# Moving the small ScalarE copies of a fused DFT and gated-cosine kernel to just ahead of the next sine

## The chip, the cores and the metric

The kernel runs on one core of one Trainium2 chip. The metric is the device time of one execution in microseconds; the median of three executions of the kernel before is 1958.15 us (1957.54 to 1958.85). Engines are named as the profile names them: PE (matrix multiply), PEld (its weight loads), DVE (vector), ACT (scalar), POOL (GpSimd), SP (the queue that issues nearly all DMAs).

## What is computed

```python
X = np.fft.fft(x, axis=1)            # x: (8, 3008, 256) fp32
X = np.fft.fft(X, axis=2)
t = X.real.astype(np.float32).reshape(24064, 256)
h = t @ w_in                         # w_in: (256, 2048)
g = h * np.cos(h)
return (g @ w_out).astype(np.float32)   # w_out: (2048, 256)
```

## The kernel before

All matrix work is in fp32. The DFT along the sequence (3008 = 47 x 64) is split in two: a first half (`first_half`, 47-point sums, 64 output rows per matrix) and a second half (`second_half`, 64-point sums with twiddles folded into the constant matrix `BJ`). The DFT along the 256 channels is folded once into `w_in`, which gives the matrices `WC` and `WS`. The real input makes one transformed row serve two output rows: `h` and its mirror.

The main loop goes over 8 batches, 6 groups of columns in each (225 columns in the first, 256 in the others), 8 pairs of feature blocks in each group. That makes 48 steps a batch, 384 in all; a step `t` has two half steps `u` = 0 and 1, numbered `k = 2t + u`. The program is written in the order in which each engine shall take its instructions, and each engine keeps that order. In one half step:

- PE: `mm1(cur, 0)` (weights `WC`), the second matrix product `mm2` of the step five half steps back, `mm1(cur, 1)` (weights `WS`), each as two instructions for one fp32 product. Both `mm1` add to a bank of PSUM that ACT has filled beforehand, the seed.
- ACT: `act_e` (L529, writes `ew`), `act_round` of the half step before (L545), `seed` of the half step to come (L498), and `act_sin` of the half step before (L555). In two half steps out of sixteen it also takes 512 columns of a finished accumulator (`take_m`, L631).
- DVE: `dve_h` (L533), `dve_frac` (L549, between rounding and sine), `dve_g` (L559, after the sine).
- POOL: `sums` (L575 to L582), combinations of finished groups, and the large parts of the folds.

While batch b is multiplied, `transform(b+1)` spreads the transform of the next batch over the 48 steps (this happens in the first seven batches; the last batch has no batch behind it). Its parts that matter here:

- `fold(b, c, e)` (L221 on) makes sums and differences of the input rows on POOL; when `e` is 1 a small copy of the end columns follows on ACT (L234, 94x8 elements). It runs at the end of steps 7, 10, 15, 18, 23, 26, 31 and 34.
- `take_middle(b, p)` (L287): a small ACT copy of the middle column into `xm` (L289, 94x8), at the end of steps 7, 8, 9 and 10. `middle` multiplies `xm` in step 11, and ACT copies the product to `zm`.
- At the first half step of steps 12, 20, 28 and 36 a pair of chunks goes through `first_half` into two borrowed PSUM banks. `keep_z` (L276) copies each bank to `zs` on ACT (L279) and then patches four columns of it from `zm` with a small copy (L281, 64x4).
- `store_z` at the end of the same step sends `zs` to DRAM over the SP queue; `load_z` at the end of steps 23 and 39 brings it back transposed; `second_half` uses it at the end of steps 42 to 47.

The order of ACT in a half step of a pair is thus: `act_e`, `act_round`, `keep_z` of the first chunk with its patch, `seed`, `act_sin`, `keep_z` of the second chunk with its patch. The copies for fold and middle column come at the very end of a step, so between the sine of one half step and `act_e` of the next.

Of the kernel before, what the change touches and what calls it, by code (L numbers as in the profile page):

```python
# [20 lines left out]
N2 = 47  # L21
NJ = 24
NI = 32
IP = 4
NCH = NI // IP
XP = 2 * IP
# [82 lines left out]
def kernel(  # L109
# [7 lines left out]
    nc = tc.nc  # L117
# [93 lines left out]
        return ppool.tile([128, 512], FP, tag=f"H{(turn[0] + k) % 4}", bufs=1, name=name)  # L211


    xfs = {}
    xf0 = [spool.tile([128, 2 * IP * 128], FP, tag="S", bufs=3, name="xf") for _ in range(2)]
    for xf in xf0:
# [2 lines left out]
    def fold(b, c, e):  # L219
        lo = IP * (c % 2)  # L220
        xv = xs[b, c // 2].rearrange("r (i d) -> r i d", d=ND)[0 : 2 * N2, lo : lo + IP]  # L221
        if b == 0:
            xfs[b, c] = xf0[c % 2]
        elif e == 0:
            xfs[b, c] = spool.tile([128, 2 * IP * 128], FP, tag="xf", bufs=2, name="xf")
        fv = xfs[b, c].rearrange("r (e i d) -> r e i d", e=2, d=128)[0 : 2 * N2]
        (nc.gpsimd if b else nc.vector).tensor_tensor(
            out=fv[:, e, :, 1:128],
            in0=xv[:, :, 1:128],
            in1=xv[:, :, 255:128:-1],  # L230
            op=ALU.subtract if e else ALU.add,
        )
        if e:
            (nc.scalar.copy if b else nc.gpsimd.tensor_copy)(  # L234
                out=fv[:, :, :, 0].rearrange("r e i -> r i e"), in_=xv[:, :, 0:129:128]
            )

    zss = {}

# [36 lines left out]
    def keep_z(b, c, pz):  # L276
        tag, n = ("zs", 4) if b or c < 4 else ("pq", 8)
        zs = spool.tile([128, 512], FP, tag=tag, bufs=n, name="zs")
        nc.scalar.copy(out=zs, in_=pz)  # L279
        if b:  # L280
            nc.scalar.copy(out=zs[64:128, 0:512:128], in_=zm[64:128, IP * c : IP * c + IP])  # L281
        zss[b, c] = zs

    xm = cpool.tile([128, NI], FP, tag="xm", name="xm")
    zm = cpool.tile([128, NI], FP, tag="zm", name="zm")

    def take_middle(b, p):  # L287
        xv = xs[b, p].rearrange("r (i d) -> r i d", d=ND)[0 : 2 * N2]
        nc.scalar.copy(out=xm[0 : 2 * N2, XP * p : XP * p + XP], in_=xv[:, :, 128])  # L289

    def clear_middle():
        pm = borrow("pm", 1)[64:128, 0:NI]
# [75 lines left out]
    def spread_nb():  # L368
        pq, nb = ready[0, 0]
        T = _width(0)  # L370
        pn = psum("pn", "M")
        nc.tensor.matmul(pn[:, 0:T], lhsT=ones, rhs=pq[0:1, T : 2 * T], start=True, stop=True)
        nc.scalar.copy(out=nb[:, 0:T], in_=pn[:, 0:T])
# [5 lines left out]
    def transform(b):  # L379
        todo = {}  # L380

        def at(o, *call):
            todo.setdefault(o, []).append(call)

        for p in range(4):
            at(2 * p, load_x, b, p)
            at(7 + p, take_middle, b, p)
            for k in range(4):
                at(8 * p + (6, 7, 9, 10)[k], fold, b, 2 * p + k // 2, k % 2)
            pairs[per * (b - 1) + 8 * p + 12] = b, 2 * p  # L390
            for c in (2 * p, 2 * p + 1):
                at(8 * p + 12, store_z, b, c)
        middles.add(per * (b - 1) + 11)
        at(23, load_z, b, 0)
        at(39, load_z, b, 1)
        for g in range(NG):
            at(42 + g, second_half, b, g)
        return todo
# [3 lines left out]
    def fold_weights(e, n, tag="M"):  # L402
        keep_weights(e, n, weights(e, n, tag))

    def weights(e, n, tag="M"):
        pw = psum("pw", tag)
        for i in range(2):
            nc.tensor.matmul(  # L408
                pw,
                lhsT=CS[i][:, 128 * e : 128 * e + 128],  # L410
                rhs=wr[n // 2][i][:, 512 * (n % 2) : 512 * (n % 2) + 512],
                start=(i == 0),
                stop=(i == 1),
            )
        return pw
# [8 lines left out]
    def weight_row(n):  # L424
        row = WS[0:1, 512 * n : 512 * n + 512]
        pw = psum("pw", "M")
        for k in range(4):
            nc.tensor.matmul(
                pw[:, k : k + 1],
                lhsT=row[:, 128 * k : 128 * k + 128],  # L430
                rhs=ones[:, 0:1],
                start=True,
                stop=True,
            )
        return pw
# [66 lines left out]
    def seed_first(h):  # L502
        s, T = h.s, h.s.T
        nc.tensor.matmul(
            h.H[:, 0:T],
            lhsT=wrow[:, 128 * h.u : 128 * h.u + 128],
            rhs=s.pq[0:1, T : 2 * T],
            start=False,
            stop=True,
            skip_group_check=True,  # L510
        )

    def mm1(h, e):
        s, T = h.s, h.s.T
        W = WS if e else WC
        f = 2 * s.fp + h.u
        nc.tensor.matmul(  # L517
            h.H[:, 0:T],
            lhsT=W[:, 128 * f : 128 * f + 128],
            rhs=s.pq[:, e * T : e * T + T],  # L520
            start=False,
            stop=True,
            skip_group_check=True,
        )

    def act_e(h):
        T = h.s.T
        h.ew = spool.tile([128, 256], FP, tag="ew", bufs=2, name="ew")
        nc.scalar.mul(out=h.ew[:, 0:T], in_=h.H[:, 0:T], mul=2.0)  # L529
# [290 lines left out]
    def step(t, last=None):  # L820
        s = steps[t] if 0 <= t < n else None
        return s if s is not None and (last is None or s.fp == 7) else None
# [3 lines left out]
    def unit(k):  # L826
        return halves[k] if 0 <= k < 2 * n else None
# [7 lines left out]
    for k in range(2 * n + LAG):  # L835
        t, u = divmod(k, 2)
        d, v = divmod(k - LAG, 2)
        cur, prev, old, nxt = unit(k), unit(k - 1), unit(k - 2), unit(k + 1)
        done = step(d)
        full = step(d if v else d - 1, True)  # L840
        if cur:
            if k % (2 * per) == 0:
                todo = transform(cur.s.b + 1) if cur.s.b + 1 < NB else {}
            if k not in range(3, AHEAD):
                mm1(cur, 0)
                if t == 0:
                    seed_first(cur)
                act_e(cur)
            if k == 0:
                spread_nb()  # L850
                fold_weights(1, 3)
            elif k == 1:
                pw = weights(0, 3)
            elif k == 2:
                pw = weight_row(3)
        pair = None if u else pairs.pop(t, None)
        if pair:
            b, c = pair
            pz = [first_half(b, c, borrow("pz"))]
        if old:  # L860
            dve_g(old)
            if old.u:
                sums(old.s)
        if pair:
            pz.append(first_half(b, c + 1, borrow("pz", 1)))
        pm = clear_middle() if u and t in middles else None
        if done:
            order = (0, 1, 5, 4, 3, 2, 6) if done is steps[-1] else range(7)
            mm2(done, 4 * v, 4 * v + 3, order)
        if pm is not None:  # L870
            middle(pm)
        if full and full is not steps[-1]:
            take_m(full, 1 if v else 3, nc.vector)
        if nxt and 0 < k < AHEAD - 1:
            seed(nxt)
        if prev:
            act_round(prev)
        if pm is not None:
            nc.scalar.copy(out=zm[64:128], in_=pm)
        if pair:  # L880
            keep_z(b, c, pz[0])
        if nxt and k >= AHEAD - 1:
            seed(nxt)
        if full and full is not steps[-1]:
            take_m(full, 0 if v else 2, nc.scalar)
        if prev:
            dve_frac(prev)
        if k + 1 in range(3, AHEAD):
            mm1(nxt, 0)
            act_e(nxt)  # L890
        if prev:
            act_sin(prev)
        if pair:
            keep_z(b, c + 1, pz[1])
        if k == 1:
            keep_weights(0, 3, pw)
        elif k == 2:
            keep_wn(3, pw)
        if cur:
            mm1(cur, 1)  # L900
        if done and v == 0:
            mm2(done, 3, 4, order)
        if cur:
            dve_h(cur)
        if u == 0:
            continue
        for i in range(6):
            s = step(t - 4 - i, True)
            if s:
                combine_m(s, i)  # L910
        for sg, lag in ((0, 8), (1, 10)):
            s = step(t - lag, True)
            if s:
                store_out(s, sg)
        for call in opening.pop(t, ()):
            call[0](*call[1:])
        for call in todo.pop(t % per, ()):
            call[0](*call[1:])
# [31 lines left out]
```

## Time and profile before

| | |
|---|---|
| median of three executions | 1958.15 us |
| the profiled execution, its own time | 1957.18 us |
| its span, first to last instruction | 1955.4 us |
| mean granted PE clock | 0.999 |
| PE busy | 1940.8 us, 99% |
| PEld busy | 1686.2 us, 86% |
| ACT busy | 1516.3 us, 78% |
| DVE busy | 1455.8 us, 74% |
| POOL busy | 1396.4 us, 71% |
| L234 copies on ACT (fold) | 56, mean 192 ns |
| L289 copies on ACT (middle column) | 28, mean 191 ns |
| L281 copies on ACT (patch of z) | 56, mean 194 ns |

The span and some 1.8 us around it make up the time of an execution. PE is busy almost throughout, and a busy PE can still lose time: the record of a matmul grows when its weights arrive late. The weight loads on PEld are shown by themselves, with the time that they stood idle and what ended it.

### The profile page before, as it was taken

How to read it: one execution, taken by the hardware profiler on the slowest of the kernel's cores; microseconds unless marked ns; L12 is line 12 of the kernel's file. 1: busy time of each engine (PE TensorE's matmuls, PEld its weight loads, DVE VectorE, ACT ScalarE, POOL GpSimd, SP SyncE). 2: the span in 40 equal slices, each digit the busy share in tenths (PEclk: the TensorE clock that was granted, in tenths of full speed). 3: DMA queues.
4: the chain of work that ended last, by engine and by line, in shares of the span. 5: the costliest groups of instructions: out<-in, count | busy, mean ns of one | idle time of the engine just before them, and what ended most of it. 6: DMA issues, size and time to landing. Idle time of an engine off the chain costs nothing.

```text
span 1955.4 us, 29697 instructions
## 1 busy us (share of the span) xinstructions
PE 1940.8 (99%) x9262; PEld 1686.2 (86%) x9262; DVE 1455.8 (74%) x2529; ACT 1516.3 (78%) x3450; POOL 1396.4 (71%) x1593
## 2 busy tenths in 40 slices
PE   9999999999999999999999999999999999999998
PEld 4888888888988889888898888988889888898887
DVE  3767777777777777777777777777777777788886
ACT  3777778777787787877778787788777877778775
POOL 3777767787577876787667776687767777666775
PEclk9999999999999999999999999999999999999999
DMA  8511124011230223201241111411114111100001
GB/s 199 126 32 39 23 54 78 21 36 39 49 68 18 41 41 64 47 22 40 41 80 29 38 28 41 86 24 41 27 36 86 23 38 28 38 22 16 12 16 28
DMA packets 176690, 88.70 MB, mean 45 GB/s; under 512 B 103303, under 2 KB 173622, under 8 KB 174902
## 3 DMA queue, kind: packets, MB, share of 16 engines
q1 hardware_dynamic: 176374, 86.68, 21.5%
q8 instruction: 75, 1.23, 0.3%
q14 instruction: 81, 0.66, 0.1%
q10 hardware_dynamic: 160, 0.13, 0.0%
HBM read 49.50 MB, written 37.27 MB: 44 GB/s over the span
## 4 chain that ended last, share of the span: by engine, by line
PE 97%; DMA 1%; ACT 0%; DVE 0%; SPq 0%; issue 0%; POOL 0%; POOLq 0%; ACTq 0%
PE M L608 58%; PE H L517 33%; PE pz L253 3%; PE pb L341 2%; DMA xp<-in_x_dram 1%; PE pw L408 0%; DMA wr<-in_moe_w_in_dram 0%; DMA nb<-nd 0%; DMA nd<-pq 0%; PE pz L250 0%; PE pm L298 0%; PE pd L464 0%; DVE r L549 0%; ACT H L498 0%; ACT r L555 0%
## 5 line engine op out<-in xcount | busy, mean ns | idle before, releaser
L575 POOL TENSOR_TENSOR S<-r 128x512 f32<-128x512 f32 (+1 forms) x383 | 474.8, 1240 | 453.0 <-DVE r L559 408.1
L555 ACT ACTIVATE r<-r 128x512 f32<-128x512 f32 (+1 forms) x768 | 477.5, 622 | 257.4 <-DVE r L549 254.5
L549 DVE SCALAR_TENSOR_TENSOR r<-r,H 128x512 f32<-128x512 f32 (+1 forms) x768 | 518.9, 676 | 199.0 <-ACT r L545 174.6
L559 DVE SCALAR_TENSOR_TENSOR r<-H,r 128x512 f32<-128x512 f32 (+1 forms) x768 | 519.2, 676 | 132.5 <-ACT r L555 92.5
L608 PE MATMUL M<-S,VX 128*128 128x256 f32 (+1 forms) x2304 | 615.7, 376 | 0.0
L608 PEld LDWEIGHTS M<-S,VX 128*128 128x128 f32 x2304 | 435.8, 190 | 70.9 <-issue 22.7
L517 PE MATMUL H<-pq,WC 128*128 128x256 f32 (+1 forms) x1536 | 455.7, 378 | 3.1 <-ACT H L498 2.9
L517 PE MATMUL H<-pq,WS 128*128 128x256 f32 (+1 forms) x1536 | 451.5, 376 | 0.0
L545 ACT ACTIVATE r<-H 128x512 f32<-128x512 f32 (+1 forms) x768 | 447.6, 583 | 0.0
L533 DVE TENSOR_TENSOR H<-ew,H 128x256 f32<-128x256 f32 (+1 forms) x768 | 324.8, 423 | 140.5 <-PE H L517 81.6
L608 PE MATMUL M<-r,w 128*128 128x256 f32 (+1 forms) x1536 | 387.8, 375 | 0.0
L498 ACT ACTIVATE H<-nb,wn 128x256 f32<-128x256 f32 (+1 forms) x766 | 365.8, 478 | 2.7 <-DMA nb<-nd 1.3
L529 ACT ACTIVATE ew<-H 128x256 f32<-128x256 f32 (+1 forms) x768 | 287.3, 374 | 98.2 <-PE H L517 94.4
L608 PEld LDWEIGHTS M<-r,w 128*128 128x128 f32 x1536 | 300.4, 197 | 27.0
L517 PEld LDWEIGHTS H<-pq,WC 128*128 128x128 f32 x1536 | 279.3, 190 | 50.1 <-ACT H L498 18.0
L517 PEld LDWEIGHTS H<-pq,WS 128*128 128x128 f32 x1536 | 290.2, 190 | 33.3 <-ACT ew L529 1.1
L581 POOL TENSOR_TENSOR S<-S,r 128x256 f32<-128x256 f32 (+1 forms) x383 | 275.5, 719 | 30.0
L582 POOL TENSOR_TENSOR S<-r,S 128x256 f32<-128x256 f32 (+1 forms) x383 | 274.5, 717 | 30.0
L608 PE MATMUL M<-S,w 128*128 128x256 f32 (+1 forms) x768 | 225.4, 375 | 0.0
L608 PE MATMUL M<-r,VX 128*128 128x256 f32 (+1 forms) x768 | 225.4, 375 | 0.0
L608 PEld LDWEIGHTS M<-S,w 128*128 128x128 f32 x768 | 150.6, 196 | 14.5
L608 PEld LDWEIGHTS M<-r,VX 128*128 128x128 f32 x768 | 146.0, 190 | 14.4
(74 smaller groups left out, 925.9 us busy)
## 6 DMA issues: line engine op xcount, KB each, us to landing
out_dram<-ob SPq DMA_DIRECT2D x728, 32.0 KB
xp<-in_x_dram SPq DMA_DIRECT2D x56, 256.0 KB
zd<-zs SPq DMA_DIRECT2D x112, 96.0 KB
z<-zd SPq DMA_DIRECT2D x28, 384.0 KB
xp<-in_x_dram SPq DMA_DIRECT2D x56, 120.0 KB
nb<-nd SPq DMA_DIRECT2D x40, 128.0 KB
wr<-in_moe_w_in_dram SPq DMA_DIRECT2D x8, 256.0 KB
w<-in_moe_w_out_dram SPq DMA_DIRECT2D x4, 512.0 KB
```

What stands on the lines that cost most here:

```text
L498: nc.scalar.activation(out=h.H[:, 0:T], in_=s.nb[:, 0:T], func=AF.Copy, bias=0.25, scale=wn[:, f : f + 1])
L517: nc.tensor.matmul(h.H[:, 0:T], lhsT=W[:, 128 * f : 128 * f + 128], rhs=s.pq[:, e * T : e * T + T], start=False, stop=True, skip_group_che ...
L529: nc.scalar.mul(out=h.ew[:, 0:T], in_=h.H[:, 0:T], mul=2.0)
L533: nc.vector.tensor_tensor(out=h.H[:, T : 2 * T][:, ::-1], in0=h.ew[:, 0:T], in1=h.H[:, 0:T], op=ALU.subtract)
L545: nc.scalar.activation(out=r, in_=y, func=AF.Copy, bias=BIG, scale=1.0)
L549: nc.vector.scalar_tensor_tensor(out=r, in0=r, scalar=-BIG, in1=y, op0=ALU.add, op1=ALU.subtract)
L555: nc.scalar.activation(out=r, in_=r, func=AF.Sin, bias=0.0, scale=SIN_SCALE)
L559: nc.vector.scalar_tensor_tensor(out=r, in0=y, scalar=-0.25, in1=r, op0=ALU.add, op1=ALU.mult)
L575: tt(out=sv[:, 0:2], in0=qv[:, 1:2].to_broadcast([128, 2, T]), in1=qv[:, 0:4:3], op=ALU.subtract,)
L581: tt(out=sv[:, 2], in0=sv[:, 1], in1=gv[:, 0, 0], op=ALU.subtract)
L582: tt(out=sv[:, 3], in0=gv[:, 1, 0], in1=sv[:, 2], op=ALU.add)
L608: nc.tensor.matmul(acc[key][m // 2][:, 256 * (m % 2) : 256 * (m % 2) + T], lhsT=w, rhs=a, start=first, stop=s.fp == 7, skip_group_check=True,)
```

## The change

The small copies for fold and middle column are no longer issued where they are called; their operands are put into a list `small`. A new function `copy_small` issues whatever the list holds, once per half step, after the seed (and `take_m`) and right in front of the sine. The two patches of a pair are taken out of `keep_z` and put into the same list after both chunks of the pair are kept, so that they are issued in the following half step. No instruction is added or taken away. The order on DVE and POOL stays as it was.

```diff
+    small = []
+
+    def copy_small():
+        for ends in small:
+            nc.scalar.copy(**ends)
+        small.clear()
+
...
         if e:
-            (nc.scalar.copy if b else nc.gpsimd.tensor_copy)(
-                out=fv[:, :, :, 0].rearrange("r e i -> r i e"), in_=xv[:, :, 0:129:128]
-            )
+            ends = dict(out=fv[:, :, :, 0].rearrange("r e i -> r i e"), in_=xv[:, :, 0:129:128])
+            if b:
+                small.append(ends)
+            else:
+                nc.gpsimd.tensor_copy(**ends)
...
         nc.scalar.copy(out=zs, in_=pz)
-        if b:
-            nc.scalar.copy(out=zs[64:128, 0:512:128], in_=zm[64:128, IP * c : IP * c + IP])
         zss[b, c] = zs
+
+    def patch_z(b, c):
+        small.append(
+            dict(out=zss[b, c][64:128, 0:512:128], in_=zm[64:128, IP * c : IP * c + IP])
+        )
...
     def take_middle(b, p):
         xv = xs[b, p].rearrange("r (i d) -> r i d", d=ND)[0 : 2 * N2]
-        nc.scalar.copy(out=xm[0 : 2 * N2, XP * p : XP * p + XP], in_=xv[:, :, 128])
+        small.append(dict(out=xm[0 : 2 * N2, XP * p : XP * p + XP], in_=xv[:, :, 128]))
...
+        copy_small()
         if prev:
             act_sin(prev)
         if pair:
             keep_z(b, c + 1, pz[1])
+            patch_z(b, c)
+            patch_z(b, c + 1)
```

## The prediction

> **What bounds the kernel now.** I read the busy shares and the chain of work first, then the waits of the weight loads, one batch at a time, then the timeline at the places they point to.
>
> ```profile
> PE 1940.8 (99%) x9262; PEld 1686.2 (86%) x9262; DVE 1455.8 (74%) x2529; ACT 1516.3 (78%) x3450; POOL 1396.4 (71%) x1593
> ...
> PE 97%; DMA 1%; ACT 0%; DVE 0%; SPq 0%; issue 0%; POOL 0%; POOLq 0%; ACTq 0%
> ```
>
> PE sets the end. ACT, whose order changes, has 22% of the span free, so an edit on it counts only where PE stands still for it. The idle column of PE would put that near zero, but a matmul whose weights came late is recorded as a longer matmul. So I look at the weight loads that waited for ACT's seed (line 498). First a whole batch in mid run (1243.5 to 1482 us), then the last batch (1720 to 1945 us), which does the same multiplications but has no next batch to transform, hence none of the small copies:
>
> ```profile
> PEld H L517 <- ACT H L498: 1.9, 8, 0.4
> ```
>
> ```profile
> PEld H L517 <- ACT H L498: 0.8, 4, 0.3
> ```
>
> Columns: total us, times, longest. Eight late seeds against four: the last batch is a control. Four of the eight fall in steps 11, 19, 27 and 35 (steps counted within the batch), each right after a step that ended with a fold copy. ACT in step 19 of the second batch, and the weight loads and matmuls that wait for it:
>
> ```profile
> 372.24 0.63 ACT L555 ACTIVATE r<-r 128x512 f32<-128x512 f32 x1
> 372.78 0.19 ACT L234 COPY xf<-xp 94x8 f32<-94x8 f32 x1
> 372.88 0.37 ACT L529 ACTIVATE ew<-H 128x256 f32<-128x256 f32 x1
> 373.15 0.58 ACT L545 ACTIVATE r<-H 128x512 f32<-128x512 f32 x1
> 373.63 0.47 ACT L498 ACTIVATE H<-nb,wn 128x256 f32<-128x256 f32 x1
> 374.48 0.63 ACT L555 ACTIVATE r<-r 128x512 f32<-128x512 f32 x1 [0.39 <-DVE r L549]
> ```
>
> ```profile
> 374.14 0.30 PEld L517 LDWEIGHTS H<-pq,WC 128*128 128x128 f32 x2 [0.23 <-ACT H L498]
> ```
>
> ```profile
> 374.15 0.69 PE L517 MATMUL H<-pq,WC 128*128 128x256 f32 x2
> ```
>
> The step before held `take_m`, so ACT is behind; the fold copy sits in its queue between the sine and `ew`; everything behind it up to the seed is that much later; the load starts when the seed is done, and the two matmuls last 0.69 us. Further, ACT then stands idle for 0.39 us ahead of the sine, waiting for DVE. The same step of the last batch, without the copy:
>
> ```profile
> 1803.10 0.60 PE L517 MATMUL H<-pq,WC 128*128 128x256 f32 x2
> ```
>
> **The change, part by part.** No instruction is added or removed: 56 + 28 + 56 = 140 copies of 0.19 us move within ACT's queue.
>
> *Fold copies at steps 18, 26, 34.* In the queue such a copy costs less than its length, for neighbours overlap: by the trace's nanoseconds it starts at 372.780 and `ew` at 372.875, so 0.095 us. Taken away there, `ew` can start at 372.78, since the matmul that it reads ended at 372.59 and the sine ahead of it overlaps a successor in the same way (in the control, sine at 1801.19, `ew` at 1801.73, 0.54 apart). The seed and the load move up by 0.095. PE lost there 0.315 - 0.216 = 0.10 us between its two matmuls, so 0.095 comes back and 0.005 stays. The distance from step 19 to step 20 says the same: 4.849 us here, 4.754 in the last batch. This loss is found at step 19 in six batches, at 27 and 35 in seven: 20 x 0.095 = 1.9 us.
>
> *Fold and middle copies at step 10.* Two copies stand in the queue there (570.48 and 570.57, then `ew` at 570.675 where 570.476 would do): 0.199 us. PE loses 0.18 + 0.105 = 0.29 us at step 11, in six batches; the same place in the last batch loses 0.09. So 0.20 x 6 = 1.2 us; the first batch loses only 0.10 there, which goes as well. Together 1.3 us.
>
> *Middle copies at steps 8 and 9, fold copies at 7, 15, 23, 31.* Nothing: no weight load of the following step waits longer than in the control (0.02 us in both, steps 9 and 10).
>
> *Patches.* In a pair's half step ACT ran `keep_z` (576.86, 0.58 long), patch (577.48), seed (577.69). Now the seed itself has to wait for `keep_z`, as it overwrites the bank which that reads, so it starts about where the patch did, 0.22 us earlier, not 0.6. PE loads for that seed at 579.21 and it was done at 578.17: no gain. The second patch stood before an `ew` that waited 0.53 us for PE anyway: no gain. 28 pairs, 0 us.
>
> *Where they go.* In front of a sine which waits for DVE's `frac`. Of the 14 half steps of a batch that now hold small copies (20 copies, 98 half steps in all), the idle time ahead of the sine in the same place is 0.39 us in eight, 0.32 in step 8, 0.33 in step 10 (0.16 in the first batch) and 0.25 in the four that follow a pair. Two copies come in at step 8, at step 11 (0.39 free) and behind each pair, elsewhere one.
>
> Price of a copy in the slot, unknown in this place: from below 0.092 (570.476 to 570.568, a copy behind a copy), from above its full 0.194. Two make 0.20 (0.092 + 0.107) to 0.39. I take the lower, as it was measured for the same two copies in the same queue; it fits everywhere, so 0 us. At the upper end only the slot behind a pair overflows, by 0.14 us, and the `ew` that comes next on ACT waits for PE in the neighbouring rows; behind the late sine on DVE stands `dve_g`, then POOL's sums, which PE takes up 3.9 us (median) after they are done. So 0 us too, unless that cover is missing (third rival).
>
> *Who reads the copies later.* The fold copy of step 10 is now done at about 571.8, read by PE at 575.7. The middle copy: one matmul of `middle` gets a wait on it, at 573.95, 2 us behind it. The patches are done about 2 us later, so the four `store_z` issues of a pair wait 2 us longer in the SP queue; for the last pair of the second batch they went out at 459.4 to 462.1 and the next entry of the queue, an output store, at 479.1. `load_z`, at 483.8, stands behind that store and does not move. 0 us.
>
> Sum: -1.9 - 1.3 = -3.2 us. The profiled execution (span 1955.4, 1.8 around it, 1957.18 in all) lies 1.0 below the median of 1958.15; I apply the difference to the median: 1954.9 us, and a span of 1952.2.
>
> A page of the Trainium skill bears on where this gain is looked for. Perfetto Trace Analysis, section Identifying the Most-Contended Engine, holds that matmul busy time is a poor measure of PE, since pipelined instructions look smaller in the trace. The trace agrees in a way of its own: the page of the profile gives PE idle for ACT's seed as 2.9 us in the whole run, the weight loads' waits for it 18.0 us; by the idle time alone the sum would have been 0.
>
> **Rivals.**
>
> *More than that.* The waits for seeds at steps 3 and 43 (0.20 and 0.06 us lost a batch, 1.9 us in seven) and the 0.09 left at step 11 (0.6) shrink too, because ACT keeps a lead. Time: 1954.9 - 1.9 = 1953.0, down to 1952.4. For: all are waits on the same queue. Against: the last batch has those at steps 3 and 11 without any small copy, and at 43 it is the copy of `pq` (0.59 us) that is in the way, which stays.
>
> *No change.* PE gains 0.1 us at a step and waits it out at the next, for POOL's sums or DVE; or the copies do not leave the path, since each half step's ACT work is the same. Time 1958.15. For: ACT's work is equal. Against: half steps behind 19, 27 and 35 run at 4.748 us a step in all batches, the matmuls' own pace, so nothing else stops PE there; and the sums are 3.9 us early.
>
> *Slower: the sine before a pair.* The second `first_half` of a pair writes into a bank that `dve_g` of two half steps before must have read; its weight load is released by DVE in 28 cases (11.1 us of idle time, hidden so far). At 576.314 it was released; PE needed it by some 576.49: 0.18 us of room. If copies at the head of ACT's queue hold the sine back by more than that, and the delay lasts over the one half step between, each pair pays the rest. With two copies at 0.19 and nothing hidden, 0.38 - 0.18 = 0.20 us, 28 times: 5.6 us, and the 0.1 us gains are gone with it: 1963.8. It decides from a delay of 0.18 us at the sine of the half step before a pair. For: it is the tightest DVE wait in the trace. Against: copies come two half steps ahead of such a sine, where 0.39 us are free. The Trainium skill's page TensorE: Matmul & The Clock Gate calls ScalarE's queue a strict FIFO of 8 in its first table; by that rule a copy ahead of the sine would hold it back whenever it is late, which is this rival.
>
> **How the numbers follow.** Forecast 0.56, more 0.24, no change 0.10, slower 0.10. 0.2% of the median is 3.9 us, about what a measurement of this kernel can tell from no change: faster means under 1954.2, slower over 1962.1. The forecast's own spread is 1954.0 to 1956.0 (step 11 or one of the three others failing, 0.7 to 1.2; the run-to-run spread of 0.65 either way), and some 0.06 of it falls below 1954.2. So faster 0.30, same 0.60, slower 0.10. The range reaches down to the first rival's 1953.0 and up to a gain of a third, 1957.1: 1952.9 to 1957.2.
>
> **What would show it.** The waits of weight loads on the seed in a mid-run batch fall from 8 to 5, and from 1.9 to about 1.0 us; the two matmuls of step 19 take 0.60 us; steps 19, 27, 35 last 4.754 us, step 11 5.39 instead of 5.59; the idle time of ACT ahead of the sine (254.5 us in the page) falls by some 10 to 25 us. A sine behind small copies that starts later than `frac` releases it, a longer wait of `pz` loads on DVE, or more than 4.75 us for a plain step would prove me wrong.

## The result and the profile after

The changed kernel takes 1955.55 us (median of 22 runs, 1953.93 to 1960.30); the kernel before takes 1958.58 (22 runs, 1956.99 to 1960.43). The ratio is 0.9986 with a 95% interval of 0.998 to 0.9993: 2.7 us less, between 1.4 and 3.9 (the two medians are 3.0 apart).

The page of the changed kernel, whose line numbers are about 12 higher (the copies of `copy_small` are L218, the seed L510, the first matrix product L529, the sine L567):

```profile
span 1953.2 us, 29669 instructions
...
PE 1939.2 (99%) x9262; PEld 1686.3 (86%) x9262; DVE 1456.8 (75%) x2529; ACT 1509.7 (77%) x3450; POOL 1396.3 (71%) x1593
...
L567 ACT ACTIVATE r<-r 128x512 f32<-128x512 f32 (+1 forms) x768 | 477.0, 621 | 242.5 <-DVE r L561 237.4
```

The same row before:

```profile
L555 ACT ACTIVATE r<-r 128x512 f32<-128x512 f32 (+1 forms) x768 | 477.5, 622 | 257.4 <-DVE r L549 254.5
```

Nothing has left any engine's queue: each engine has as many instructions as in the page before. The idle time of ACT ahead of the sine, released by DVE, fell from 254.5 to 237.4 us: the copies stand in it now. The waits of the weight loads for the seed, in the stretch of a mid-run batch that corresponds to the one shown before (1242.4 to 1480.4 us), and in the last batch (1718 to 1943 us):

```profile
PEld H L529 <- ACT H L510: 1.0, 5, 0.3
```

```profile
PEld H L529 <- ACT H L510: 0.8, 4, 0.3
```

Eight waits have become five; the last batch, which has no small copies in either kernel, is as it was. Step 19 of the second batch, ACT in the timeline, then the two matmuls that had taken 0.69 us:

```profile
372.77 0.63 ACT L567 ACTIVATE r<-r 128x512 f32<-128x512 f32 x1
373.31 0.36 ACT L541 ACTIVATE ew<-H 128x256 f32<-128x256 f32 x1
373.57 0.59 ACT L557 ACTIVATE r<-H 128x512 f32<-128x512 f32 x1
374.05 0.48 ACT L510 ACTIVATE H<-nb,wn 128x256 f32<-128x256 f32 x1
374.45 0.20 ACT L218 COPY xf<-xp 94x8 f32<-94x8 f32 x1
374.92 0.63 ACT L567 ACTIVATE r<-r 128x512 f32<-128x512 f32 x1 [0.27 <-DVE r L561]
```

```profile
374.68 0.60 PE L529 MATMUL H<-pq,WC 128*128 128x256 f32 x2
```

`ew` now starts 0.54 us behind the start of the sine, not 0.64; the copy has gone behind the seed, and the sine is still released by DVE, after 0.27 us of idle time where there had been 0.39. The sine is not late.

The times of single runs scatter by more than the gain, but the distance from one step to the next (the first matmul of L517, or L529, of each) repeats within about 0.01 us in the middle of the run (step 35 of the fourth batch and step 27 of the seventh are 0.10 to 0.14 longer than their neighbours in every kernel). All readings below use it; of the kernels in the table behind the first two, each ran once, apart from the two with the seed first (10 and 5 runs). What each of them changes stands with its experiment. The fifth batch, in us:

| kernel | batch | step 11 | 12 | 13 | 19 | 20 | 27 | 28 | 35 | 43 |
|---|---|---|---|---|---|---|---|---|---|---|
| before | 238.50 | 5.587 | 6.824 | 4.750 | 4.846 | 6.815 | 4.846 | 6.813 | 4.847 | 5.705 |
| changed | 238.03 | 5.387 | 6.825 | 4.748 | 4.757 | 6.813 | 4.757 | 6.813 | 4.757 | 5.706 |
| folds and middle only | 238.03 | 5.386 | 6.825 | 4.749 | 4.757 | 6.813 | 4.754 | 6.814 | 4.755 | 5.707 |
| patches only | 238.50 | 5.581 | 6.825 | 4.748 | 4.846 | 6.814 | 4.847 | 6.813 | 4.847 | 5.707 |
| folds only | 238.12 | 5.473 | 6.825 | 4.748 | 4.755 | 6.813 | 4.757 | 6.813 | 4.754 | 5.706 |
| copies three times | 240.42 | 6.107 | 6.825 | 5.036 | 4.753 | 6.814 | 4.754 | 6.813 | 4.753 | 5.706 |
| changed, seed first | 239.06 | 5.759 | 6.825 | 4.749 | 4.749 | 7.026 | 4.749 | 7.024 | 4.748 | 5.663 |
| before, seed first | 239.58 | 5.969 | 6.825 | 4.749 | 4.811 | 7.060 | 4.812 | 7.061 | 4.814 | 5.665 |
| changed, 8 dummies | 238.89 | 5.384 | 7.349 | 4.748 | 4.754 | 6.929 | 4.756 | 6.931 | 4.753 | 5.706 |
| changed, 14 dummies | 241.28 | 5.381 | 7.939 | 4.748 | 4.755 | 7.525 | 4.759 | 7.522 | 4.754 | 5.707 |

Batches 2 to 7 take 2.90 us less in the changed kernel than before. From the start of the second batch to the end of the span it is 1672.28 against 1669.38 us; the opening and the first batch go the other way, 283.10 against 283.83.

### The profile page after: what moved, and what is told of

It is laid out like the page before. It is cut to its first block, busy times and chain, and to the rows that moved or that the text cites. A ratio compares the mean times of both kernels' runs of the same rounds, so it can differ in the third digit from the quotient of the medians.

```text
span 1953.2 us, 29669 instructions
## 1 busy us (share of the span) xinstructions
PE 1939.2 (99%) x9262; PEld 1686.3 (86%) x9262; DVE 1456.8 (75%) x2529; ACT 1509.7 (77%) x3450; POOL 1396.3 (71%) x1593
## 4 chain that ended last, share of the span: by engine, by line
PE 98%; ACT 0%; DMA 0%; DVE 0%; SPq 0%; POOL 0%; issue 0%; POOLq 0%; ACTq 0%
PE M L620 58%; PE H L529 33%; PE pz L262 3%; PE pb L353 2%; PE pw L420 1%; DMA xp<-in_x_dram 0%; PE pz L259 0%; PE pw L440 0%; DMA wr<-in_moe_w_in_dram 0%; PE pm L310 0%; PE pd L476 0%; DVE r L561 0%; ACT r L567 0%; POOL xf L245 0%; DVE cb L687 0%; ACT r L557 0%
## 5 line engine op out<-in xcount | busy, mean ns | idle before, releaser
L567 ACT ACTIVATE r<-r 128x512 f32<-128x512 f32 (+1 forms) x768 | 477.0, 621 | 242.5 <-DVE r L561 237.4
L529 PE MATMUL H<-pq,WC 128*128 128x256 f32 (+1 forms) x1536 | 453.6, 377 | 2.1 <-ACT H L510 2.1
L529 PE MATMUL H<-pq,WS 128*128 128x256 f32 (+1 forms) x1536 | 451.5, 376 | 0.0
L510 ACT ACTIVATE H<-nb,wn 128x256 f32<-128x256 f32 (+1 forms) x766 | 366.3, 478 | 0.9
L529 PEld LDWEIGHTS H<-pq,WS 128*128 128x128 f32 x1536 | 290.3, 190 | 33.7 <-ACT ew L541 1.0
L529 PEld LDWEIGHTS H<-pq,WC 128*128 128x128 f32 x1536 | 279.2, 190 | 45.9 <-ACT H L510 11.0
```

The costliest lines, as they stand in the source:

```text
L510: nc.scalar.activation(out=h.H[:, 0:T], in_=s.nb[:, 0:T], func=AF.Copy, bias=0.25, scale=wn[:, f : f + 1])
L529: nc.tensor.matmul(h.H[:, 0:T], lhsT=W[:, 128 * f : 128 * f + 128], rhs=s.pq[:, e * T : e * T + T], start=False, stop=True, skip_group_che ...
L567: nc.scalar.activation(out=r, in_=r, func=AF.Sin, bias=0.0, scale=SIN_SCALE)
```

## The experiments

**Which copies carry the gain.** Three kernels with a part of the change each.

Folds and middle column only:

```diff
         nc.scalar.copy(out=zs, in_=pz)
+        if b:
+            nc.scalar.copy(out=zs[64:128, 0:512:128], in_=zm[64:128, IP * c : IP * c + IP])
         zss[b, c] = zs
...
-            patch_z(b, c)
-            patch_z(b, c + 1)
```

> The change without its part for z: the patches stay inside keep_z, the copies for fold and middle column go ahead of the sine. Read by the distance from step to step in the trace, batches 2 to 7. My theory: the whole gain is here, steps 11, 19, 27 and 35 as in the changed kernel (5.387 and 4.756 us against 5.586 and 4.849 before), 0.48 us a batch. Rival (patches carry a part of it): less than 0.48 us a batch, or other steps that are longer than in the changed kernel.

Measured: 238.03 us a batch, no step of batches 2, 3, 5, 6 or 8 off by more than 0.015 us from the changed kernel, and of batches 4 and 7 by no more than 0.025. The whole gain is in these copies. Steps 9, 10, 16, 24 and 32, which follow the other small copies, are as in the kernel before, here and in the changed kernel.

Patches only:

```diff
-            if b:
-                small.append(ends)
-            else:
-                nc.gpsimd.tensor_copy(**ends)
+            (nc.scalar.copy if b else nc.gpsimd.tensor_copy)(**ends)
...
-        small.append(dict(out=xm[0 : 2 * N2, XP * p : XP * p + XP], in_=xv[:, :, 128]))
+        nc.scalar.copy(out=xm[0 : 2 * N2, XP * p : XP * p + XP], in_=xv[:, :, 128])
```

> The other part alone: patches go half a step later and ahead of the sine, the copies for fold and middle column stay at the end of their step. My theory: no step changes by more than 0.01 us, 0.00 us a batch, although the seed in a pair's half step starts about 0.2 us earlier. Rival (the earlier seed helps): the step of a pair (6.81 us) or the one behind it gets shorter.

Measured: batches 2 to 8 within 0.015 us of the kernel before. In the pair's half step the seed does start earlier: by the trace's nanoseconds 0.618 us after `keep_z` where it had been 0.835 (577.693 less 576.858), in the changed kernel as here. PE has no use for it. This part of the change is worth nothing.

Folds only (the first kernel, and `take_middle` copies at once as before):

```diff
-        small.append(dict(out=xm[0 : 2 * N2, XP * p : XP * p + XP], in_=xv[:, :, 128]))
+        nc.scalar.copy(out=xm[0 : 2 * N2, XP * p : XP * p + XP], in_=xv[:, :, 128])
```

> Fold copies alone go ahead of the sine; middle column and patches stay as before. My theory prices a copy in the queue by its start-to-start time: steps 19, 27 and 35 as in the changed kernel (4.756), step 11 in between, about 5.49 us (one of two copies gone, 0.09 to 0.107 of 0.199). Rival (a copy costs its whole length, or the pair of copies costs as one): step 11 at 5.39 or unchanged at 5.59.

Measured: step 11 at 5.473 to 5.482, about half way between 5.587 and 5.387; 19, 27 and 35 as in the changed kernel. ACT ahead of that step, in the timeline of this run:

```profile
571.46 0.63 ACT L569 ACTIVATE r<-r 128x512 f32<-128x512 f32 x1
572.00 0.19 ACT L303 COPY xm<-xp 94x8 f32<-94x8 f32 x1
572.09 0.37 ACT L543 ACTIVATE ew<-H 128x256 f32<-128x256 f32 x1
```

One copy of 0.19 us holds `ew` back by 0.09. That, not its length, is its price in the queue, and each of the two copies at step 10 has such a price of its own.

**How much room there is ahead of the sine.** Every small copy three times:

```diff
         for ends in small:
-            nc.scalar.copy(**ends)
+            for _ in range(3):
+                nc.scalar.copy(**ends)
```

> The changed kernel with each small copy issued three times in a row ahead of the sine. Three in a slot of 0.39 us should just fit (3 x 0.095 + 0.1); six overflow it by about 0.3 us at steps 8 and 11 and by about 0.4 us behind a pair. My theory: the sine starts that much later there and PE does not notice, since ACT waits for PE again before the next seed: batches stay within 0.1 us of the changed kernel's 238.03. Rival (a late sine costs PE what it is late): some 0.3 us in each of six half steps, 1.5 to 2 us a batch.

Measured: 2.4 us more a batch. The expected price of three copies and the conclusion that PE would not notice both failed. ACT behind a pair:

```profile
587.25 0.48 ACT L511 ACTIVATE H<-nb,wn 128x256 f32<-128x256 f32 x1
587.76 1.19 ACT L219 COPY zs<-zm 64x4 f32<-64x4 f32 x6
588.98 0.63 ACT L568 ACTIVATE r<-r 128x512 f32<-128x512 f32 x1
```

Six copies take 1.19 us: a copy that writes the same place as the one just before it starts only 0.225 us behind it (587.757, 587.982, 588.207), while copies with outputs of their own follow in 0.09 to 0.11. So three copies overflow the slot too: at steps 16, 19, 24, 27, 32 and 35 the sine is 0.11 to 0.12 us late, without a loss there. Behind a pair the sine starts 1.725 us after the seed where the changed kernel has 0.868, so 0.86 late, and step 13 is 0.29 longer. Cover exists there, some 0.57 us; it is not without end. At steps 8 to 11 the losses add to 1.28 us (step 11 alone 0.72).

**The rival with the sine before a pair.** Dummy copies, each into columns of its own, ahead of the sine of the half step before each pair:

```diff
+    pad = cpool.tile([128, 8 * 16], FP, tag="pad", name="pad")
+    nc.vector.memset(pad, 0.0)
...
         copy_small()
+        if u and t + 1 in pairs:
+            for i in range(8):
+                nc.scalar.copy(out=pad[:, 8 * i : 8 * i + 8], in_=w2[:, 0:8])
         if prev:
             act_sin(prev)
```

> The changed kernel with eight small copies into a scratch tile, each to columns of its own, ahead of the sine of the half step before each pair: the sine there starts about 0.3 us late at steps 19, 27 and 35, 0.75 late at step 11. My theory (cover of about 0.6 us behind a late sine, from the run with copies issued three times): no loss at 20, 28 and 36, at most 0.2 us at step 12. Rival (the third of the prediction: the second first_half has 0.18 us of room behind dve_g): 0.1 us and more at steps 20, 28 and 36, 0.5 at step 12.

> The same with fourteen copies: the sine before a pair about 0.85 us late at steps 19, 27, 35, 1.3 late at step 11. My theory: about 0.25 us lost at 20, 28 and 36, 0.7 at step 12. Rival (0.18 us of room): 0.65 us lost at each of 20, 28, 36, 1.1 at step 12, and the pz weight loads wait for dve_g.

Measured with eight: `dve_g` ends 1.445 us behind the start of the pair's half step where it had been 1.132, so 0.31 later, and steps 20, 28 and 36 are 0.12 longer, step 12 0.52. With fourteen it ends at 2.04, 0.91 later, and the steps are 0.71 and 1.11 longer. My theory (cover as behind a pair) failed; the rival's law holds: at steps 20, 28 and 36 the loss is the lateness less 0.20 us (0.31 - 0.12, 0.91 - 0.71). At step 12 `dve_g` is 0.79 and 1.38 late and the room is 0.27 us. The weight loads of `first_half` in the pair at step 20 of the third batch say by what. Before the dummies (changed kernel), with eight, with fourteen:

```profile
615.84 0.20 PEld L262 LDWEIGHTS pz<-xf,L 94*64 94x64 f32 x4 [0.33 <-DVE H L545]
616.50 0.39 PEld L262 LDWEIGHTS pz<-xf,L 94*64 94x64 f32 x4 [0.46 <-DVE r L571]
```

```profile
618.44 0.20 PEld L262 LDWEIGHTS pz<-xf,L 94*64 94x64 f32 x4 [0.33 <-DVE H L547]
619.41 0.20 PEld L262 LDWEIGHTS pz<-xf,L 94*64 94x64 f32 x4 [0.78 <-DVE r L573]
```

```profile
623.00 0.20 PEld L262 LDWEIGHTS pz<-xf,L 94*64 94x64 f32 x4 [0.33 <-DVE H L547]
624.58 0.20 PEld L262 LDWEIGHTS pz<-xf,L 94*64 94x64 f32 x4 [1.38 <-DVE r L573]
```

The second chunk's first load waits for `dve_g` in all three; 0.66, 0.97 and 1.58 us pass between the chunks. In the changed kernel the wait is there, but PE's matmuls of the first chunk are still running when it ends.

**A seed that goes first.** The losses left after the change sit at steps 3, 11 and 43, where the seed is late too. So the seed was put ahead of the rounding in the half step behind both `take_m` (the first one of steps 3, 11, 19, 27, 35 and 43), in the changed kernel and in the kernel before:

```diff
+        early = nxt and k >= AHEAD and t % 8 == 3 and u == 0
+        if early:
+            seed(nxt)
         if prev:
             act_round(prev)
...
-        if nxt and k >= AHEAD - 1:
+        if nxt and k >= AHEAD - 1 and not early:
             seed(nxt)
```

> The changed kernel, and in the first half step of steps 3, 11, 19, 27, 35 and 43 of each batch (the half step after both take_m) the seed goes ahead of act_round. My theory: the losses that the change leaves (0.20 us at step 3, 0.09 at 11, 0.06 at 43) come from a late seed, so step 3 falls from 4.395 to about 4.19, step 11 from 5.387 to 5.30, step 43 from 5.705 to 5.64: 0.35 us a batch, 237.7 us, and about 2.5 us less than the changed kernel in all, ratio to the kernel before about 0.9973. Rival (these steps are short of ACT as a whole): rounding and sine are 0.4 us later instead and the loss shows at the same or the next step, batches of 238.0 us or more.

> The kernel before, all small copies where they were, with the same swap of seed and act_round in those half steps. My theory (a copy costs only where the seed behind it is late): steps 19, 27, 35 fall to about 4.75 and step 11 to about 5.30 without any copy being moved, batches of about 237.7 us, the same as with the change. Rival (a copy in the queue costs by itself): steps 19, 27, 35 stay near 4.85 and 238.2 us or more a batch.

Measured: 1962.54 us, ratio 1.0022 (1.0012 to 1.0031), and 1966.06 us, ratio 1.004 (1.0027 to 1.0052). Both are slower than before, and both theories failed. The waits for the seed fell all the same, over the whole run; the waits of `first_half` for `dve_g` grew, and so did those of the middle product (`pm`) for DVE and of the first product for `ew`. The changed kernel, then the same with the seed first:

```profile
PEld H L529 <- ACT H L510: 11.0, 42, 1.5
PEld pz L262 <- DVE r L571: 11.0, 28, 0.5
...
PEld pm L310 <- DVE pm L305: 2.3, 7, 0.3
...
PEld H L529 <- ACT ew L541: 1.0, 3, 0.3
```

```profile
PEld pz L262 <- DVE r L571: 19.6, 28, 0.9
...
PEld H L529 <- ACT H L510: 6.6, 20, 1.5
PEld pm L310 <- DVE pm L305: 5.4, 7, 0.8
...
PEld H L529 <- ACT ew L541: 5.0, 20, 0.4
```

The rounding goes behind the seed, and one half step further on the sine is still 0.40 us late (2.776 us behind the half step's start against 2.376); the pair that follows pays 0.21, again the lateness less 0.2. Step 43, with no pair behind it, gains 0.04. Step 3 is 0.02 longer and step 4 0.065: in step 3 of the third batch a weight load waits 0.32 us for `ew` where one had waited 0.29 for the seed. Step 11 loses 0.37: the load of the middle product waits 0.80 us for DVE where it had waited 0.33. In the kernel before, the swap takes 0.035 off steps 19, 27 and 35, not the 0.09 that moving the copies gives. So a place where the seed is late is not by itself a place to gain: what is moved ahead of the rounding is paid where the later sine holds up other work, here `dve_g` and the clearing of `pm` behind it on DVE, and `ew` behind it on ACT.

## Why the prediction was right

*Fold copies at steps 18, 26 and 34.* Predicted 20 times 0.095, 1.9 us. Measured: steps 19, 27 and 35 shorter by 0.09 to 0.10 in the same 20 places, 1.84 us together.

*Fold and middle copies at step 10.* Predicted 0.20 in six batches and 0.10 in the first, 1.3 us. Measured 0.193 to 0.202 and 0.12: 1.31 us. The run with folds alone divides it into two halves.

*The control.* That the last batch, without small copies, shows what stays was the firmest step: after the change batches 2 to 7 have 4.755 to 4.757 at step 19, where the last batch had 4.754 before.

*Patches at nothing, in both places.* Right, shown by the run with patches alone. The seed's new wait was priced right as well (0.22 us earlier).

*The price in the slot.* Predicted 0.092 from below, 0.194 from above, the lower taken. The idle time ahead of the sine went from 0.39 to 0.27 us with one copy (0.33 to 0.26 at step 10), from 0.39 to 0.17 and 0.32 to 0.105 with two, from 0.25 to 0.07 with two patches: 0.07 to 0.12 each, and it fits everywhere. The idle time fell by 17 us, forecast 10 to 25. The working at the upper price missed two places: two copies of 0.19 us would have overflowed the 0.32 at step 8 as well, by 0.07, and one the 0.16 at step 10 of the first batch, by 0.03. It did not matter, as the lower price came out. That an overflow of 0.14 would have cost nothing was not tried at that size; 0.11 at steps 16 to 35 cost nothing in the run with three copies, and cover of 0.2 us before a pair and some 0.57 behind one was measured.

*More than forecast.* Did not come: steps 3 and 43 and the rest at step 11 are unchanged to 0.01 us, and the swap shows that they can't be had from the seed's place alone.

*No change.* Excluded by the interval, and by step distances that keep what they gain.

*Slower.* The mechanism exists, with about the size that was given: 0.18 us of room was read from the pair of step 12, where 0.27 came out, and 0.20 at the other three pairs of a batch. It did not decide because the sine before a pair is not held back (`dve_g` ends 1.132 us behind the half step's start after the change, 1.140 before).

*The sum.* 3.2 us forecast; 2.90 measured in batches 2 to 7, where the terms give 2.9 as well (0.485 each), and 0.3 in steps 11, 27 and 35 of the first batch. That makes the 3.2. The time of 1954.9 was counted from a median of three runs, 1958.15; over 22 runs the kernel before takes 1958.58, so 0.4 of the 0.65 us between forecast and measurement lies there. The times alone put the gain between 1.4 and 3.9 us, so that they come this near is partly luck; the step distances carry the proof.

The two profiled spans differ by 2.2 only, because the opening went the other way: its third step took 4.84 us before and 6.52 after, its eighth 5.13 and 4.19. The third step has the same instructions in both kernels, and the clock explains its length: the granted PE clock was 0.5 from 50.6 to 54.0 us in the changed kernel's trace, and full there in the one before. Half the clock for 3.4 us is the 1.7 us. In the eighth step before, the seed on ACT waited 1.3 us for a DMA (`nb`); after, it did not. In the ten traces the third step took 4.84 us in the four with the full clock there, and 6.40 to 7.48 in the six with a clock of 0.5 for 3.4 or 6.8 us. The change can hardly be its cause: the first small copy on ACT comes later (at 76.0 us in the trace before), the run with eight dummies has the moved copies and the full clock, and 4 of 14 runs of the kernel before have the mean clock of 0.997 that goes with 6.8 us in these traces. What makes the clock fall there stays open.

## What to carry to other kernels

When the bounding engine shows hardly any idle time, look at the waits of its weight loads stretch by stretch, and find a stretch that lacks the work in question: here it gave the gain before any run did. A small instruction on an engine that feeds it belongs where that engine waits for a third one, and costs nothing there as long as it fits; how far it may overflow is set by the tightest reader of what stands behind it, here 0.20 us. Moving the late instruction itself forward, past one whose result feeds another chain, shifted the loss to that chain and made it larger.

## What the runs showed of the hardware that was not expected

Small ACT copies that follow one another start 0.09 to 0.11 us apart when each writes a place of its own, also when all read the same input, as the dummies do. They start 0.22 to 0.24 us apart when they write the same place; two patches issued three times each filled 1.19 us, which spoilt the size of one experiment.

Where PEld stood idle for 0.23 us ahead of a late weight load, PE lost only 0.10 us; where it stood idle for 0.42, PE lost 0.29. In the records of this kernel the first 0.13 us cost nothing, as the matmuls before the load were still running.

In the opening the granted PE clock fell to 0.5 for 3.4 or 6.8 us in six of the ten traces, and equal matmuls then started 0.37 us apart where they had started 0.19 apart. The scatter of single runs goes partly with it: 14 runs of the kernel before have a median of 1957.42 us at a mean clock of 0.999 (4 runs), 1958.61 at 0.998 (6) and 1959.70 at 0.997 (4).
